# Weight-gradient products moved from the end of a backward pass in among its earlier weight products

## Chip, cores, metric

One core of one Trainium2 chip. The metric is device microseconds (us) of one execution. "Before" is the kernel as found, "after" the changed one. Most executions of one kernel lie within about 1% of each other. Each ratio here compares runs of the same call on the same chip. Where two changed kernels run at different times are set side by side, only their ratios to before are strictly comparable. In "1192 us (1187 to 1196)" the first number is the median and the brackets hold the lowest and highest run.

## The reference, cut to what matters

The program runs two layers of attention and MLP with shared weights, for two rows of activations, forward and backward, and returns the output and nine gradients.

```
# D = 1024, F = 3584, 32 query heads, 4 KV heads of 128, 16384 cached keys, batch 2
x = x + A(layernorm(x))     # attention over a cache, then @ wo
x = x + B(layernorm(x))     # gelu(y @ w1 + b1) @ w2 + b2
x = x + A(layernorm(x))     # same weights again
x = x + B(layernorm(x))
out, vjp = jax.vjp(...)     # gradients of x, k_cache, v_cache, wq, wo, w1, b1, w2, b2
```

A weight gradient is an outer product summed over four rows (two layers, two batch rows). dW2, dW1 and dWo are 23 MB in bf16: little arithmetic, many bytes to store.

## The kernel before

In what follows PE is the matrix engine (TensorE) and PEld its loading of stationary operands, DVE is VectorE, ACT is ScalarE, POOL is GpSimd. PSUM is the memory that TensorE writes to; an "eviction" copies a result from PSUM to the working memory SBUF.

The kernel streams weights and caches (348 MB read, 99 MB written). After 700 us come, in this order:

1. **w1**: for layer 0, w1 is loaded, transposed on TensorE and multiplied by `dh_all` into `dm`;
2. **ln**: two layernorm backwards, with transposes ("turns") of wo rows between their steps, up to `gA_all`;
3. **wo products**: wo times `gA_all`;
4. **loop**: delta of layer 0 and the first pass over kept keys and values, the score loop;
5. **tail**: the rest of the K and V gradients, dWq, and before the change also all of dW2, dW1 and dWo.

In the w1 stage a "push" transposes up to eight blocks into PSUM, copies them to SBUF and multiplies the push of two steps ago:

```
def push(self, wv, j, jj, o0, on):                       # class BwdPipe, cut
    tp = (pt if self.n % 3 else px)([128, 8, 128], BF16, "wtp")
    for o in range(on):
        PE.transpose(tp[:, o, :], wv[:, j, (o0 + o) * 128:(o0 + o + 1) * 128], ident[:])
    wT = ktp.tile([128, 8, 128], BF16, name="wT", tag="kT")
    evac_bf16(wT..., tp..., on * 128)                    # on ScalarE or VectorE
    ...                                                  # then the matmuls of an older wT
```

A gradient "unit" is one product of 4 rows x 128 columns by 4 rows x 512 columns into one PSUM bank, plus one eviction into a 1 MB tile (its "home"), which is stored when full. There are 176 of them: 56 for dW2, 56 for dW1, 64 for dWo.

```
def u(...):                                              # dw_units, cut
    if j == 0 and c0 == 0:
        box["t"] = new_home()
    ps = mx()
    PE.matmul(ps[:], lhsT=xrows[p:p + 4, ...128 columns], rhs=yrows[p:p + 4, ...512 columns],
              start=True, stop=True, tile_position=(p, 0))
    evac_cast(sv_[:, j, c0:c0 + 512], ps[:], 512)
    if j == rb - 1 and c0 + 512 >= ny:
        store(out_of(j0, rb), sv_, box["t"])
```

The stages, cut:

```
_, dmps = w_pass(B_w1, D, F, "dm_ps", gT_bf=dh_all[:, :, lsl(0)])      # w1
wob = Ahead(A_wo, HD, "wob")                                           # loads of wo
dn = ln_bwd(..., lambda: some(rest, 4)); dx = ln_bwd(...)              # ln, with turns between
for j in range(wob.J + 4): ...; wob.products(j - 4, dops, gA_all[...]) # wo products
do_delta(0, pairs(dops, HQ))
by_read = deque(ld.tile(...) for _ in range(NLD - 1))                  # load tiles, NLD = 7
fill = deque(); fill.append(rows_unit(...)); fill.append(... units of dW2, dW1, dWo ...)
for c in range(NCH): ...                                               # score loop
while ...: ...                                                         # tail: takes from fill and late
```

Of the kernel before, what the change touches and what calls it, by code (L numbers as in the profile page):

```python
# [23 lines left out]
def kernel(  # L24
# [50 lines left out]
    NLD = 7  # L75
    WIDE = 32
# [99 lines left out]
    def part_sum(src, n, name):  # L176
        ps = pm_([128, n], F32, name)
        PE.matmul(ps[:], lhsT=onesf[:], rhs=src, start=True, stop=True)
        return ps
# [8 lines left out]
    def col_to_row_f32(colT, J, dram_out, name):  # L188
        row = wrk.tile([2, J * 128], BF16, name=name + "_row", tag="rowout")
        for j0 in range(0, J, 4):  # L190
            ps = pm_([2, 4, 128], F32, name)
            for j in range(4):
                PE.transpose(ps[0:2, j, :], colT[:, j0 + j, :], identf[:])
            V.tensor_copy(out=row[:, j0 * 128:(j0 + 4) * 128], in_=ps[0:2, :, :].rearrange("p a b -> p (a b)"))
        nc.gpsimd.dma_start(dram_out, row[:])
# [57 lines left out]
    class BwdPipe:  # L253


        def __init__(self, out_ps, gT_bf, n_o):
            self.out_ps, self.gT, self.n_o, self.q, self.n = out_ps, gT_bf, n_o, deque(), 0

        def push(self, wv, j, jj, o0, on):
            self.n += 1  # L260
            tp = (pt if self.n % 3 else px)([128, 8, 128], BF16, "wtp")
# [383 lines left out]
    n_all = vec.tile([128, DJ, 4], BF16, name="n_all")  # L645
    o_all = vec.tile([128, HQ, 4], BF16, name="o_all")
    dq_all = vec.tile([128, HQ, 4], BF16, name="dq_all")
    gA_all = vec.tile([128, DJ, 4], BF16, name="gA_all")
    m_all = vec.tile([128, DJ, 4], BF16, name="m_all")
    h_all = vec.tile([128, FJ, 4], BF16, name="h_all")  # L650
    dh_all = vec.tile([128, FJ, 4], BF16, name="dh_all")
    gM_all = vec.tile([128, DJ, 4], BF16, name="gM_all")
# [86 lines left out]
    def attn_out_bwd(l, gT):  # L739
        V.tensor_copy(out=gA_all[:, :, lsl(l)], in_=gT[:])  # L740
        _, dops = w_pass(A_wo, HD, D, "do_ps", gT_bf=gA_all[:, :, lsl(l)])
        return do_delta(l, dops)

    def do_delta(l, dops):
# [5 lines left out]
        doT_bf = vec.tile([128, G, 8], BF16, name=f"doT_bf{l}")  # L750
        V.tensor_copy(out=doT_bf[:], in_=dof[:])
        prod = wrk.tile([128, G, 8], F32, name="dprod")
        V.tensor_tensor(out=prod[:], in0=dof[:], in1=sv["oT"][:], op=ALU.mult)
        dlp = part_sum(prod[:].rearrange("p g r -> p (g r)"), G * 8, "dl_ps")
        rest_ = wrk.tile([128, G * 8], F32, name="dl_rest")
        V.tensor_scalar(out=rest_[:], in0=dlp[:], scalar1=-1.0, scalar2=None, op0=ALU.mult)
# [12 lines left out]
        saved[f"a{l}"]["doT_bf"] = doT_bf  # L769
        return doT_bf  # L770
# [78 lines left out]
    x4 = mlp_out(1, fps[:, 0:DJ * WIDE].rearrange("p (j b) -> p j b", b=WIDE)[:, :, 0:2])  # L849
    col_to_row_f32(x4, DJ, out_0.rearrange("b s d -> (b s) d"), "o0")  # L850
    sv = saved["m0"]
    _, dmps = w_pass(B_w1, D, F, "dm_ps", gT_bf=dh_all[:, :, lsl(0)])
    wob = Ahead(A_wo, HD, "wob")
    for k in range(len(wob.chunks)):
        wob.load(k)
    rest = deque(lambda j=j: wob.row(j) for j in range(wob.J - 4))
    dm = wrk.tile([128, DJ, 2], F32, name="dm_sb")
    V.tensor_copy(out=dm[:], in_=dmps[:])
    dn = ln_bwd(dm[:], sv["y2"][:], sv["rstd2"][:], "dn", lambda: some(rest, 4))
    dx = ln_bwd(dn[:], sv["y1"][:], sv["rstd1"][:], "dx", lambda: some(rest, 4))  # L860
    g1 = vec.tile([128, DJ, 2], F32, name="gM0")
    V.tensor_tensor(out=g1[:], in0=dx[:], in1=g2[:], op=ALU.add)
    V.tensor_copy(out=gA_all[:, :, lsl(0)], in_=g1[:])
    dops = px([128, 512], F32, "wob_b")
    for j in range(wob.J + 4):
        some(rest, 1)
        if j >= wob.J - 4 and j < wob.J:
            wob.row(j)
        if j >= 4:
            wob.products(j - 4, dops, gA_all[:, :, lsl(0)])  # L870
    TP = [pt([128, 8, 128], BF16, "tpm%d" % i) for i in range(2)]
    for t in TP:
        V.memset(t[:].bitcast(F32), 0.0)
    do_delta(0, pairs(dops, HQ))



    rowsA = ld.tile([128, LDW], BF16, name="rowsA", tag="ld")
    rowsB = wrk.tile([128, D], BF16, name="rowsB", tag="rowout")

    def rows_unit(srcs, dst, j0):

        def u():
            tp = mtp()
            n = 0
            for i, (colT, jlo) in srcs.items():
                jn = min(8, colT.shape[1] - jlo)
                n = max(n, jn)
                for j in range(jn):
                    PE.transpose(tp[32 * i:32 * i + 4, j, :], colT[:, jlo + j, :], ident[:], tile_position=(0, 32 * i))  # L890
            lo, hi = 32 * min(srcs), 32 * max(srcs) + 4
            evac_bf16(dst[lo:hi, j0 * 128:(j0 + n) * 128], tp[lo:hi, 0:n, :].rearrange("p a b -> p (a b)"), n * 128)

        return Unit(u)

    X = [px([128, 512], F32, "xm%d" % i) for i in range(4)]
    rot = {"x": 0, "tp": 0}


    by_read = deque(ld.tile([128, LDW], BF16, name="big", tag="ld") for _ in range(NLD - 1))  # L900
    by_store = deque()

    def nxt(what, lst):
        rot[what] += 1
        return lst[(rot[what] - 1) % len(lst)]

    def mx():
        return nxt("x", X)

    def mtp():  # L910
        return nxt("tp", TP)

# [13 lines left out]
    class Unit:  # L926
        def __init__(self, f, home=False):
            self.f, self.home = f, home

        def ready(self):  # L930
            return not self.home or n_free() > 3
# [4 lines left out]
    def dbias(rows, i, n, out_ap, name):  # L936
        p = 32 * i
        row = new_home()
        for c0 in range(0, n, 512):
            ps = mx()  # L940
            PE.matmul(ps[p:p + 1, :], lhsT=ones_bf[p:p + 4, 0:1], rhs=rows[p:p + 4, c0:c0 + 512], start=True, stop=True,
                      tile_position=(p, p))
            evac_cast(row[p:p + 1, c0:c0 + 512], ps[p:p + 1, :], 512)
        store(out_ap.rearrange("(o f) -> o f", o=1), row[p:p + 1, 0:n], row)

    def dw_units(xrows, yrows, i, chunks, y0, ny, out_of):

        p = 32 * i
        box = {}
        units = []  # L950
        for j0, rb in chunks:
            for j in range(rb):
                for c0 in range(0, ny, 512):
                    def u(j0=j0, rb=rb, j=j, c0=c0):
                        if j == 0 and c0 == 0:
                            box["t"] = new_home()
                        sv_ = box["t"][:, 0:rb * ny].rearrange("p (j n) -> p j n", j=rb)
                        ps = mx()
                        PE.matmul(ps[:], lhsT=xrows[p:p + 4, (j0 + j) * 128:(j0 + j + 1) * 128],  # L959
                                  rhs=yrows[p:p + 4, y0 + c0:y0 + c0 + 512], start=True, stop=True, tile_position=(p, 0))  # L960
                        evac_cast(sv_[:, j, c0:c0 + 512], ps[:], 512)
                        if j == rb - 1 and c0 + 512 >= ny:
                            store(out_of(j0, rb), sv_, box["t"])
                    units.append(Unit(u, j == 0 and c0 == 0))
        return units

    def rows_of(out_ap):
        return lambda j0, rb: out_ap[j0 * 128:(j0 + rb) * 128, :].rearrange("(j p) n -> p j n", p=128)

# [18 lines left out]
    def load_next():  # L988
        job = jobs.popleft()
        t = loaded[job] = load_tile()  # L990
# [21 lines left out]

    pump(NLD - 1, 0)

    fill = deque()
    fill.append(rows_unit({0: (gM_all, 0), 1: (m_all, 0), 2: (gA_all, 0), 3: (n_all, 0)}, rowsB, 0))
    for j0 in range(0, HQ, 8):
        srcs = {0: (h_all, j0), 1: (dh_all, j0), 2: (o_all, j0)}
        fill.append(rows_unit({i: v for i, v in srcs.items() if j0 < v[0].shape[1]}, rowsA, j0))
    units = [dw_units(rowsA, rowsB, 0, list(w_chunks(F, D)), 0, D, rows_of(out_8)),  # L1020
            dw_units(rowsB, rowsA, 1, list(w_chunks(D, F)), 0, F, rows_of(out_6))]
    while any(units):
        for u_ in units:
            if u_:
                fill.append(u_.pop(0))
    fill.append(Unit(lambda: dbias(rowsB, 0, D, out_9, "db2"), True))
    fill.append(Unit(lambda: dbias(rowsA, 1, F, out_7, "db1"), True))
    fill.extend(dw_units(rowsA, rowsB, 2, list(w_chunks(HD, D)), 0, D, rows_of(out_5)))
# [5 lines left out]
    for w in "VK":  # L1034
        cols[w] = vec.tile([128, G, 2, 8], BF16, name="cols" + w)
        for k in range(2):
            src = saved["a%d" % k]["qT_bf" if w == "K" else "doT_bf"]
            V.tensor_copy(out=cols[w][:, :, k, :], in_=src[:])
# [82 lines left out]
    def quarter(kv):  # L1121
# [3 lines left out]
        late.append(rows_unit({3: (dq_all, kv * 8)}, rowsA, kv * 8))  # L1125
# [172 lines left out]
```

## Time and profile before

1181.67 us, median of 3 runs (1176.63 to 1184.82), at a mean granted TensorE clock of 0.827 in the profiled run, which took 1184.54 us.

The first view is the page's division of the span into 40 slices of 29.6 us. DMA is the busy share of the DMA engines in tenths, PEclk is the granted TensorE clock in tenths of full speed, GB/s is what the DMA engines moved.

```profile
PEclk9988886597989876989998998987877877786785
DMA  9999999998999989989999939767999999999996
GB/s 370 416 417 417 417 417 395 393 341 365 417 417 413 412 312 416 393 327 414 411 396 383 365 136 398 293 231 296 372 403 420 420 413 418 419 421 418 423 423 267
```

DMA is busy nine tenths or more of almost every slice, and 410 to 423 GB/s recur. The exceptions behind the middle are slices 24, 26, 27 and 28, counted from one (136, 293, 231 and 296 GB/s), that is 680 to 710 us and 740 to 829 us.

The second view gives the busy time of each engine by stretch; I cut the stretches at the stages. The columns are: stretch, its length, then busy us and instruction count of PE, PEld, DVE, ACT and POOL, then clock, DMA share, GB/s. The six rows are w1, ln, a short step from `gA_all` to the first product, wo products, loop, tail.

```profile
core 0: us, PE busy (x) PEld busy (x) DVE busy (x) ACT busy (x) POOL busy (x), PEclk, DMA share, GB/s
711.00:735.40 24.40, 21.93 (x460) 20.45 (x461) 10.81 (x20) 9.17 (x16) 0.71 (x1) 0.89 1.03 400
735.40:743.00 7.60, 6.37 (x92) 5.51 (x90) 5.51 (x24) 3.52 (x6) 0.00 (x0) 1.00 0.94 344
743.00:744.10 1.10, 1.02 (x16) 0.90 (x16) 0.64 (x2) 0.44 (x1) 0.00 (x0) 1.00 0.24 82
744.10:760.20 16.10, 16.06 (x412) 15.67 (x409) 7.27 (x11) 6.01 (x11) 0.00 (x0) 1.00 0.81 290
760.20:779.70 19.50, 13.32 (x246) 7.92 (x247) 10.55 (x33) 6.60 (x15) 0.58 (x1) 0.77 0.48 196
779.70:1182.80 403.10, 350.77 (x4505) 210.22 (x4503) 295.85 (x505) 276.01 (x527) 57.28 (x97) 0.75 0.96 389
```

In w1 the DMA is full (share 1.03, where 1 or a little over is full; 400 GB/s), though PE is also 90% busy. The wo products run at 290 GB/s and the loop at 196. The tail is bound by bytes: 403 us at 389 GB/s and a DMA share of 0.96, though the clock is only 0.75. Its loads wait for stores to give tiles back, as the largest row of the DMA queue's own waits in the tail shows (total us, times, longest):

```profile
SPq L997 <- DMA out_dram<-big: 103.1, 16, 17.5
```

### The profile page before, as it was taken

The page shows a single profiled execution, that of the slowest core. Times are in us where ns is not written, and L with a number is a line of the kernel's source. Part 1 is how long each engine was busy: PE and PEld are TensorE (multiplying, and loading weights), DVE is VectorE, ACT ScalarE, POOL GpSimd, SP SyncE. Part 2 cuts the span into 40 slices and gives each one's busy share as a digit, 9 for nine tenths or more (in the row PEclk, how much of TensorE's full clock was granted, in tenths as well). Part 3 has the DMA queues.
Part 4 walks back from the last instruction along what each step waited for, and adds up shares of the span by engine and source line. Part 5 has one row for each costly group of instructions (what it writes and reads, how often), then busy time and mean ns, then how long its engine had stood idle before and what let it go on. Part 6 is the DMA issues. An engine that isn't in the chain of part 4 may idle for free. (4 is left out here: it accounts for less than half of the span.)

```text
span 1182.8 us, 40678 instructions
## 1 busy us (share of the span) xinstructions
PE 981.7 (83%) x17981; PEld 754.3 (64%) x17981; DVE 606.4 (51%) x1264; ACT 538.2 (46%) x1366; POOL 63.9 (5%) x113
## 2 busy tenths in 40 slices
PE   4989795488879876899798988888988889999885
PEld 3867673488767756887676788755555554555552
DVE  1544351233535423444243334567877877786774
ACT  0544341022535421334233323366766867685773
POOL 0000000000000000000000000001111111111111
PEclk9988886597989876989998998987877877786785
DMA  9999999998999989989999939767999999999996
GB/s 370 416 417 417 417 417 395 393 341 365 417 417 413 412 312 416 393 327 414 411 396 383 365 136 398 293 231 296 372 403 420 420 413 418 419 421 418 423 423 267
DMA packets 89133, 449.35 MB, mean 380 GB/s; under 512 B 7026, under 2 KB 7026, under 8 KB 49788
## 3 DMA queue, kind: packets, MB, share of 16 engines
q1 hardware_dynamic: 72204, 348.17, 73.9%
q0 software_dynamic: 16752, 98.59, 20.3%
q8 instruction: 140, 2.29, 0.8%
q14 instruction: 37, 0.30, 0.1%
HBM read 348.14 MB, written 98.58 MB: 378 GB/s over the span
## 5 line engine op out<-in xcount | busy, mean ns | idle before, releaser
L148 ACT COPY kT<-tp 128x512 int32<-128x512 int32 x181 | 106.3, 587 | 266.0 <-PE tp L379 258.2
L151 DVE COPY kT<-tp 128x1024 bf16<-128x1024 bf16 x187 | 128.1, 691 | 152.7 <-PE tp L379 143.1
L379 PE MATMUL tp<-ident,kv_K 128*128 128x128 bf16 x1728 | 144.7, 233 | 4.6 <-DMA kv_K<-in_A_k_cache_dram 4.0
L379 PEld LDWEIGHTS <-kv_K 128*128 128x128 bf16 x1728 | 109.9, 104 | 5.2 <-DMA kv_K<-in_A_k_cache_dram 5.1
L159 DVE CAST big<-xm 128x512 bf16<-128x512 f32 (+1 forms) x140 | 91.0, 685 | 30.3 <-PE xm L1100 15.9
L156 ACT CAST big<-xm 128x512 bf16<-128x512 f32 (+1 forms) x157 | 85.7, 593 | 25.1 <-PE xm L959 15.1
L521 PEld LDWEIGHTS <-kT 128*128 128x128 bf16 x2048 | 76.7, 98 | 28.7 <-issue 22.9
L521 PE MATMUL sc<-qT_bf,kT 128*128 128x8 bf16 x2048 | 92.2, 171 | 0.7 <-issue 0.7
L263 PE MATMUL wtp<-ident,wt 128*128 128x128 bf16 x928 | 77.0, 231 | 3.6 <-issue 2.3
L297 PEld LDWEIGHTS <-wt 128*128 128x128 bf16 x1696 | 49.1, 103 | 46.4 <-issue 15.3
L485 ACT ACTIVATE e_all<-sc,negm 128x64 bf16<-128x64 f32 x256 | 77.1, 343 | 1.3 <-DVE negm L480 1.1
L379 PE MATMUL tp<-ident,kv_V 128*128 128x128 bf16 x864 | 69.9, 227 | 7.7 <-DMA kv_V<-in_A_v_cache_dram 6.3
L159 DVE CAST keepK<-xm 128x512 bf16<-128x512 f32 x95 | 61.7, 684 | 18.8 <-PE xm L1100 13.6
L405 PE MATMUL acc_all<-kv_V,e_all 128*16 128x256 bf16 x864 | 46.5, 295 | 29.2 <-DMA kv_V<-in_A_v_cache_dram 16.2
L148 ACT COPY wT<-wtp 128x512 int32<-128x512 int32 (+1 forms) x60 | 34.5, 576 | 78.2 <-PE wtp L263 63.4
L151 DVE COPY wT<-wtp 128x1024 bf16<-128x1024 bf16 (+1 forms) x64 | 40.5, 636 | 52.0 <-PE wtp L263 48.7
L156 ACT CAST keepK<-xm 128x512 bf16<-128x512 f32 x102 | 54.8, 592 | 19.7 <-PE xm L1100 18.9
L263 PEld LDWEIGHTS <-wt 128*128 128x128 bf16 x928 | 58.9, 103 | 4.4 <-issue 2.9
L379 PEld LDWEIGHTS <-kv_V 128*128 128x128 bf16 x864 | 54.6, 102 | 9.8 <-DMA kv_V<-in_A_v_cache_dram 7.3
L159 DVE CAST keepV<-xm 128x512 bf16<-128x512 f32 (+1 forms) x78 | 50.8, 685 | 18.8 <-PE xm L1100 14.8
L156 ACT CAST keepV<-xm 128x512 bf16<-128x512 f32 (+1 forms) x94 | 51.0, 594 | 19.8 <-PE xm L1100 16.8
L485 ACT ACTIVATION_READ_ACCUMULATOR e_all<-sc,negm 128x1 f32 x256 | 59.8, 234 | 0.0
(325 smaller groups left out, 1762.7 us busy)
## 6 DMA issues: line engine op xcount, KB each, us to landing
kv_K<-in_A_k_cache_dram SPq DMA_DIRECT2D x81, 1024.0 KB, 12.9
kv_V<-in_A_v_cache_dram SPq DMA_DIRECT2D x81, 1024.0 KB, 11.9
out_dram<-big POOLq DMA_DIRECT2D x36, 1024.0 KB, 17.0
wt<-in_A_wo_dram SPq DMA_DIRECT2D x32, 1024.0 KB, 11.1
wt<-in_B_w_dram SPq DMA_DIRECT2D x32, 896.0 KB, 14.4
out_dram<-keepK POOLq DMA_DIRECT2D x22, 1024.0 KB, 17.3
out_dram<-keepV POOLq DMA_DIRECT2D x18, 1024.0 KB, 17.2
wt<-in_A_wq_dram SPq DMA_DIRECT2D x16, 1024.0 KB, 9.1
```

Source lines behind the costliest of these rows:

```text
L148: S.copy(out=dst.bitcast(I32), in_=src.bitcast(I32))
L151: V.tensor_copy(out=dst, in_=src)
L156: S.copy(out=dst, in_=src)
L159: V.tensor_copy(out=dst, in_=src)
L263: PE.transpose(tp[:, o, :], wv[:, j, (o0 + o) * 128:(o0 + o + 1) * 128], ident[:])
L297: PE.matmul(fps[:, jo, :].rearrange("p (a b) -> p a b", b=2), lhsT=wv[:, j, jo * 128:(jo + 1) * 128], rhs=xT_bf[:, j0 + j, :].unsqueeze(1) ...
L379: PE.transpose(tp[:, j, :], cv[:, b * 8 + j, :], ident[:])
L405: PE.matmul(self.acc[cg:cg + 16, :], lhsT=coef(u), rhs=self.cv[:, t:t + 2, :].rearrange("p t d -> p (t d)"), start=False, stop=True, tile_ ...
L485: S.activation(out=e_all[:, g, f * half:(f + 1) * half, l, h, :], in_=sc[g][f][:, h, :].rearrange("p (a b) -> p a b", b=2), func=ACT.Exp, ...
L521: PE.matmul(sc[g][f][:, :, t % TH], lhsT=kT[:, j, :], rhs=q_bf[:, g, :], start=True, stop=True)
```

## The change

The intent: the tail is full of bytes and the stages before it have some room, so the gradient products and their stores go there. Three load tiles become homes early. Two units are "fed" after each w1 push and each wo turn, one after each wo product, three per step of the score loop. So that neighbouring units use different parts of the TensorE array, each operand's rows are spread over four strips of partitions (0, 32, 64, 96). The row transposes of out_0 go from ahead of w1 to ahead of the wo products. Delta of layer 0 is divided: the scaled gradient comes before the loop, the sum inside its first step. The transposes of w1 also lose the third PSUM bank that they took in turn before. No byte is added or removed. The diff, cut to its core:

```diff
+    by_read, by_store = deque(), deque(ld.tile([128, LDW], BF16, name="home", tag="ld") for _ in range(NHOME))
 ...
+                    if split == "x":
+                        p, xo, yo = 32 * (jj % 4), jj // 4 * 128, c * 512
+                    else:
+                        p, xo, yo = 32 * (c % 4), jj * 128, c // 4 * 512
+                    PE.matmul(ps[:], lhsT=x[p:p + 4, xo:xo + 128], rhs=y[p:p + 4, yo:yo + 512], start=True, stop=True,
+                              tile_position=(p, 0))
 ...
+    fill.extend(dw_units(hr, gMr, list(w_chunks(F, D)), D, rows_of(out_8), "x"))
+    feed(4)
     x4 = mlp_out(1, ...)
-    col_to_row_f32(x4, DJ, out_0.rearrange("b s d -> (b s) d"), "o0")
+    feed(4)
 ...
-    _, dmps = w_pass(B_w1, D, F, "dm_ps", gT_bf=dh_all[:, :, lsl(0)])
+            for o0 in range(0, FJ, 8):
+                pipe.push(wv, j, j0 + j, o0, min(8, FJ - o0))
+                feed(2)
 ...
+    LEAD = 4 * (NLD - NHOME)
+    def turned(j):
+        wob.row(j)
+        feed(2)
 ...
+    for j in range(wob.J):
+        if j >= LEAD // 2 and j + LEAD // 2 < wob.J:
+            wob.row(j + LEAD // 2)
+        wob.products(j, dops, gA_all[:, :, lsl(0)])
+        feed(1)
 ...
-    do_delta(0, pairs(dops, HQ))
+    prod = do_scaled(0, pairs(dops, HQ), cols["V"][:, :, 0, :])
 ...
     for c in range(NCH):                                   # score loop
+        if c == 0:
+            qv()
+            delta(0, prod, mx())
 ...
+        feed(3)
```

## The prediction

> **What bounds the kernel now.** The slices of the page show DMA at 0.9 or more of its time almost everywhere, at about 418 GB/s: the kernel is bound by moved bytes (449 MB). Summing the windows view, about 180 MB move after 700 us; at 418 GB/s that is 431 us, but it takes 482 us, so some 50 us of DMA time is idle there. It lies at 700-706 us (5), 740-750 (149 GB/s: 6), 765-790 (14), 800-825 (9, clock 0.67) and the drain after 1150 (10). The w1 products run from 713.7 to 735.5 us, wo turns and products to 760, delta to 764 (timeline). dW2, dW1 and dWo (23 MB, 55 us of DMA) all come after 811 us, where DMA is already full: loads wait for stores to free tiles (the DMA queue's waits: over 300 us on stores).
>
> **What changes.** No bytes are added or removed. 176 dW units (one 4x128x512 product, one eviction: 0.59 us on ACT or 0.69 on DVE, 372 ns on PE, partly overlapped) and their stores move forward. Counting the feeds: 8 units before w1, 64 among its 32 pushes, 32 among the first 16 wo turns, about 32 in the wo products, 12 in the score loop; some 30 stay in the tail. About 148 units, 18.5 MB, leave the tail: 44 us at 418 GB/s.
>
> **What it costs.**
> - w1: 22 us becomes 33-37: 64 evictions (41 us) plus the wT ones (18) over two engines is 30 us, at 80-90% filling. The Trainium skill (TensorEngine Tiling (Array Packing), PSUM Bottleneck) says that tiling speeds TensorE, not eviction; I expect that here: four strips help PE little, the evictions set the pace.
> - rows transposes and eight units before w1: about 3 us.
> - the 16 turns with both layernorm backwards: 18 us; out_0's transposes (3.5 us) now stand before the wo products.
> - wo products: 28-30 us, since only four tiles hold weights and the last four chunks are loaded only as products free them.
> So wo products end near 798-805 us instead of 760: 38-45 us later. DMA is near full in w1, but idles some 15-20 us in the layernorm chain and the wo products (8 there before).
>
> **What it gains back.** The tail loses 44 us. The gap at 765-780 mostly closes: delta waits inside the first score step, V gradients and dWo stores flow at once, and no clearing or rows units stand in the way (10-15 us of idle gone). One more tile is free for loads. Four instead of six loads are prefetched (-5 us). The drain is unchanged.
>
> **Sum.** 1182 + 42 - 44 - 12 (gap and rows) = about **1168 us**, range **1150 to 1187**. Faster by over 2%: 0.30; within 2%: 0.64; slower by over 2%: 0.06. So most of the 44 us is paid back by slower w1 and wo stages.
>
> **What would show it.** DMA rate in the w1 stage stays above 380 GB/s though it lasts 12 us or more longer; ACT and DVE busy there go from about 45% to 80% or more; wo products end near 800 us; a DMA trough (below 300 GB/s) in the layernorm chain and the start of the wo products, with PE waiting for the fifth wo chunk; no trough below 100 GB/s in the score loop; tail still at 415-420 GB/s, ending about 10-15 us earlier.
>
> **What would make it wrong.** Faster: evictions and PE overlap better, so w1 ends at 30 us and products by 790 (then 1150). Slower: a unit's eviction waits for its home's store (three homes, 17 us to landing in the tail) and blocks the in-order engines and so the products; or the tail turns out bound by PE (88-92% busy there at a clock near 0.75) rather than by bytes, so that taking stores out gives little.

## The result, and the profile after

After ran in 1219.27 us (1216.36 to 1225.12, 4 runs) against 1179.15 us (1176.32 to 1184.82, 4 runs) for before. Ratios here are the mean time of one kernel's fast runs over that of the other's from the same rounds, so not quite the ratio of those medians: 1.034, 95% interval 1.028 to 1.040. The change made the kernel slower; the prediction was wrong.

The 40 slices of after (30.4 us each):

```profile
PEclk9988795678898857999889965565977997796795
DMA  9999999989999989999999388457999999999965
GB/s 372 418 420 419 419 418 396 390 312 420 419 418 419 390 356 400 354 405 413 396 392 373 128 311 299 186 200 281 374 407 416 424 424 420 424 423 421 417 277 208
```

The same six stages of after:

```profile
702.30:761.20 58.90, 56.22 (x637) 37.58 (x626) 32.43 (x53) 33.22 (x60) 6.60 (x9) 0.54 0.82 303
761.20:781.50 20.30, 20.30 (x136) 12.07 (x134) 8.85 (x30) 15.15 (x29) 2.13 (x4) 0.50 0.58 234
781.50:788.50 7.00, 6.09 (x38) 3.27 (x36) 3.97 (x6) 3.37 (x6) 0.53 (x1) 0.50 0.32 131
788.50:834.90 46.40, 39.67 (x486) 24.86 (x483) 17.93 (x26) 15.94 (x28) 3.71 (x6) 0.57 0.62 216
834.90:857.40 22.50, 19.27 (x267) 8.99 (x268) 12.74 (x35) 11.07 (x23) 1.86 (x3) 0.50 0.75 278
857.40:1217.90 360.50, 281.69 (x4328) 180.88 (x4328) 248.15 (x434) 230.04 (x442) 43.69 (x76) 0.79 0.94 387
```

Differences of the two profiles, stage by stage in us:

| | start of w1 | w1 | ln | step | wo products | loop | tail | end |
|---|---|---|---|---|---|---|---|---|
| before | 711.0 | 24.4 | 7.6 | 1.1 | 16.1 | 19.5 | 403.1 | 1182.8 |
| after | 702.3 | 58.9 | 20.3 | 7.0 | 46.4 | 22.5 | 360.5 | 1217.9 |
| difference | -8.7 | +34.5 | +12.7 | +5.9 | +30.3 | +3.0 | -42.6 | +35.1 |

The tail gave back what was expected. The four stages ahead of the loop took 83.4 us more. (The start of w1 is not the change's doing for certain: over my twelve runs, whose code up to there is nearly that of after, it lay anywhere between 704 and 709 us. And each stage is read from one execution: the profiled one of before, at 1184.54 us, was 5 us above before's median.)

What stands out is the clock. In w1 PE is busy 56.2 of 58.9 us, at 0.54 of full speed; before it was 0.89. In stretches of 5 us it reads as follows. First after: in w1, in ln, two in the wo products, and at the start of the tail:

```profile
715.00:720.00 5.00, 5.00 (x52) 3.58 (x51) 2.63 (x5) 2.78 (x6) 0.77 (x1) 0.50 0.92 366
775.00:780.00 5.00, 5.00 (x35) 3.10 (x34) 3.12 (x5) 3.27 (x7) 0.53 (x1) 0.50 0.52 210
795.00:800.00 5.00, 0.51 (x1) 0.00 (x1) 0.38 (x1) 0.59 (x1) 0.00 (x0) 0.50 1.01 356
810.00:815.00 5.00, 4.92 (x102) 3.64 (x100) 2.57 (x4) 2.77 (x5) 0.00 (x0) 1.00 0.60 213
860.00:865.00 5.00, 4.43 (x77) 3.07 (x78) 4.22 (x8) 3.61 (x8) 0.00 (x0) 1.00 0.99 391
```

Then before, in w1 and at the wo products:

```profile
720.00:725.00 5.00, 5.00 (x123) 4.89 (x119) 2.23 (x4) 2.81 (x5) 0.00 (x0) 1.00 1.01 394
745.00:750.00 5.00, 5.00 (x121) 4.92 (x118) 2.21 (x5) 2.32 (x4) 0.00 (x0) 1.00 0.46 107
```

In after, PE shows no idle time in these stretches of w1 and ln, and yet keeps half its clock. Apart from 7 us it is back at 1.00 only from about 858 us on, when the tail begins (whose mean is 0.79). (By stage it is 0.50 to 0.57 from w1 to the loop.) In those 7 us the trace shows what was different: from 806.7 to 811.4 us PE ran transposes and wo products alone, no gradient product, and at 810 us the clock went to 1.00; then a gradient product came every 1.1 us or so, PE idled for 0.6 us, and at 817 us the clock was at 0.50 again. In before the clock is 1.00 in both. The page's groups, restricted to w1, show the cost for single operations (busy us, mean ns). First after (lines between left out), then before:

```profile
L265 PE MATMUL wtp<-ident,wt 128*128 128x128 bf16 x224 | 29.7, 310 | 0.0
...
L955 PE MATMUL xe<-gMr,hr 4*128 4x512 bf16 x56 | 16.4, 569 | 1.7 <-ACT home L157 0.9 <-ACT hr L149 0.7
```

```profile
L263 PE MATMUL wtp<-ident,wt 128*128 128x128 bf16 x224 | 18.1, 227 | 0.0
```

The same 224 transposes have a mean of 310 ns instead of 227, and a gradient product lasts 569.

### The profile page after: what moved, and what is told of

It reads as the page before. It is cut to its first block, busy times and chain, and to the rows that moved or that the text cites. A ratio compares the mean times of both kernels' runs of the same rounds, so it can differ in the third digit from the quotient of the medians.

```text
span 1217.9 us, 41059 instructions
## 1 busy us (share of the span) xinstructions
PE 995.2 (82%) x18149; PEld 761.5 (63%) x18149; DVE 600.4 (49%) x1261; ACT 545.2 (45%) x1377; POOL 63.8 (5%) x113
## 3 DMA queue, kind: packets, MB, share of 16 engines
q0 software_dynamic: 16752, 98.59, 19.8%
## 5 line engine op out<-in xcount | busy, mean ns | idle before, releaser
L265 PE MATMUL wtp<-ident,wt 128*128 128x128 bf16 x928 | 91.2, 256 | 3.3 <-issue 2.0
L265 PEld LDWEIGHTS <-wt 128*128 128x128 bf16 x928 | 68.4, 115 | 18.2 <-issue 16.8
L299 PEld LDWEIGHTS <-wt 128*128 128x128 bf16 x1696 | 49.0, 103 | 45.0 <-issue 14.7
L381 PE MATMUL tp<-ident,kv_V 128*128 128x128 bf16 x864 | 67.4, 222 | 7.4 <-DMA kv_V<-in_A_v_cache_dram 6.4
L407 PE MATMUL acc_all<-kv_V,e_all 128*16 128x256 bf16 x864 | 46.4, 294 | 29.1 <-DMA kv_V<-in_A_v_cache_dram 17.7
L157 ACT CAST home<-xe 128x512 bf16<-128x512 f32 (+1 forms) x84 | 47.7, 586 | 46.6 <-PE xe L955 40.0
L149 ACT COPY wT<-wtp 128x512 int32<-128x512 int32 (+1 forms) x58 | 32.9, 568 | 61.4 <-PE wtp L265 51.7
L160 DVE CAST keepK<-xm 128x512 bf16<-128x512 f32 x80 | 51.5, 684 | 16.7 <-PE xm L1155 11.5
L149 ACT COPY kT<-tpm 128x512 int32<-128x512 int32 x65 | 38.7, 595 | 45.2 <-PE tpm L1305 45.0
L160 DVE CAST home<-xe 128x512 bf16<-128x512 f32 (+1 forms) x57 | 39.2, 690 | 37.1 <-PE xe L955 35.0
L157 ACT CAST keepK<-xm 128x512 bf16<-128x512 f32 x88 | 47.3, 592 | 14.7 <-PE xm L1155 10.7
L160 DVE CAST big<-xm 128x512 bf16<-128x512 f32 x64 | 41.5, 684 | 23.0 <-PE xm L1155 21.0
## 6 DMA issues: line engine op xcount, KB each, us to landing
kv_V<-in_A_v_cache_dram SPq DMA_DIRECT2D x81, 1024.0 KB, 12.7
```

The source lines that it names most:

```text
L149: S.copy(out=dst.bitcast(I32), in_=src.bitcast(I32))
L157: S.copy(out=dst, in_=src)
L160: V.tensor_copy(out=dst, in_=src)
L299: PE.matmul(fps[:, jo, :].rearrange("p (a b) -> p a b", b=2), lhsT=wv[:, j, jo * 128:(jo + 1) * 128], rhs=xT_bf[:, j0 + j, :].unsqueeze(1) ...
L381: PE.transpose(tp[:, j, :], cv[:, b * 8 + j, :], ident[:])
L407: PE.matmul(self.acc[cg:cg + 16, :], lhsT=coef(u), rhs=self.cv[:, t:t + 2, :].rearrange("p t d -> p (t d)"), start=False, stop=True, tile_ ...
```

## Experiments

Theory A: the thin products (4 of 128 rows) keep TensorE's granted clock at one half although it is busy, and PE so becomes the pace of w1, ln and wo. The Trainium skill ("TensorE: Matmul & The Clock Gate", Part 1, What's actually happening) says that the clock is throttled by default and released by activity, with half and full as the two states, and that a sustained busy window of about 3.4 us is enough to release it. That an instruction which is busy all the time might not count fully is not in that section; that is what had to be tested.

Rival B: it is the switching between the strips and the whole array. The skill ("TensorEngine Tiling (Array Packing)", Key Properties) says that a change of tiling mode drains TensorE; on such a story the clock is a symptom.

Rival C: evictions and homes are the pace, as the prediction held, and the low clock is only what an engine gets that waits.

Theory D, besides, which the expectations name from run 8 on: feeding early is a loss in itself, because w1's DMA was already full.

### 1. Products over all 128 rows (results of dW wrong, on purpose)

```diff
-PE.matmul(ps[:], lhsT=x[p:p + 4, xo:xo + 128], rhs=y[p:p + 4, yo:yo + 512], start=True, stop=True,
-          tile_position=(p, 0))
+PE.matmul(ps[:], lhsT=x[:, xo:xo + 128], rhs=y[:, yo:yo + 512], start=True, stop=True)
```

The number of products, evictions, homes and bytes is unchanged. (One small memset of rows that nothing else writes is added; runs 5, 6 and 7 have it too.)

> Changed kernel, but every dW product multiplies all 128 rows of its operand tiles instead of 4 (dW2, dW1, dWo, dWq come out wrong on purpose; same count of products, columns, evictions, bytes). Theory A (the clock): products that use 4 of 128 rows leave the array looking idle, so TensorE is granted half its clock (0.55 in w1, 0.50 to 0.57 to the end of the wo products) and paces these stages. Then here: granted clock above 0.9 in the w1 stage, w1 stage 34 to 40 us instead of 59, wo products 30 to 36 instead of 47, total 1170 to 1190 us. Rival B (switching between 32-row strips and the whole array costs time by itself): faster too, since nothing switches any more, so this run alone does not part A from B. Rival C (evictions and waits for home tiles set the pace): no change, 1219 us, w1 59 us.

Measured: 1191.94 us (1186.55 to 1196.29) beside 1179.93 (1177.25 to 1183.22) for before, ratio 1.009 (1.006 to 1.013). Stages w1 and wo products, then the two groups of w1 again:

```profile
708.60:757.80 49.20, 40.99 (x646) 28.75 (x635) 32.21 (x55) 32.22 (x60) 6.65 (x10) 0.93 0.97 360
776.60:812.20 35.60, 27.74 (x486) 21.00 (x484) 17.75 (x26) 15.64 (x28) 3.10 (x6) 0.81 0.68 229
```

```profile
L265 PE MATMUL wtp<-ident,wt 128*128 128x128 bf16 x224 | 19.1, 229 | 0.0
L955 PE MATMUL xe<-gMr,hr 128*128 128x512 bf16 x56 | 17.8, 389 | 4.4 <-DVE home L160 3.0 <-ACT hr L149 0.7 <-ACT home L157 0.5
```

The clock is 0.93 in w1 and the products, though 32 times as many rows, last 389 ns instead of 569. Some 27 of the 40 us are gone. But w1 still takes 49 us where theory A had forecast 34 to 40, the total misses its range by 2 us, and now the DMA is full in w1 (0.97), at 360 GB/s.

### 2. Products over 32 rows (wrong, on purpose)

```diff
-lhsT=x[p:p + 4, ...], rhs=y[p:p + 4, ...]
+lhsT=x[p:p + 32, ...], rhs=y[p:p + 32, ...]        # same tile_position=(p, 0)
```

> Changed kernel with every dW product on all 32 rows of its strip instead of 4 (dW wrong on purpose); the strips and the switching stay. A, if what counts is how many rows work: between the changed kernel and the full-row run, clock in w1 0.6 to 0.9, total 1185 to 1212 us. B: no change, 1219 us, clock in w1 0.55, since the switching is the same. C: no change.

Measured: 1214.01 us (1205.63 to 1216.42), ratio 1.027 (1.023 to 1.031). w1:

```profile
704.30:764.20 59.90, 56.81 (x641) 37.99 (x627) 32.42 (x53) 33.12 (x60) 6.58 (x9) 0.53 0.80 296
```

Nearly as after: filling one strip helps neither the clock nor w1. This is what B and C had forecast; theory A, in the form that more rows give more clock step by step, missed both its clock and its total.

### 3. No products until the wo products have ended (wrong, on purpose)

```diff
+if late_stage:
     PE.matmul(ps[:], lhsT=x[p:p + 4, ...], rhs=y[p:p + 4, ...], start=True, stop=True, tile_position=(p, 0))
-evac_cast(sv_[:, j, c * 512:(c + 1) * 512], ps[:], 512)
+evac_cast(sv_[:, j, c * 512:(c + 1) * 512], ps[:] if late_stage else ACCT[:], 512)
```

Evictions and stores stay where after has them; they read an idle PSUM bank.

> Changed kernel without the dW products up to the end of the wo products: their evictions, stores and waits for home tiles stay, but read the idle accumulator bank (those dW wrong on purpose). A and B: clock 0.9 to 1.0, w1 stage 32 to 38 us (evictions then set the pace: about 30 us of busy time on each of two engines), wo products 28 to 34, total 1165 to 1185 us. C: w1 stays near 59 us and the total near 1219 us.

Measured: 1196.42 us (1191.73 to 1200.89), ratio 1.013 (1.010 to 1.017). w1:

```profile
704.40:754.90 50.50, 32.14 (x579) 29.40 (x568) 30.48 (x54) 30.92 (x61) 6.95 (x10) 0.71 0.97 364
```

With the products gone and all evictions left, w1 falls from 59 to 50 us, as with full rows. So rival C can claim at most 50 us of w1, not the 59. The forecast of A and B (32 to 38 us in w1, total 1165 to 1185) was missed too; only the wo products, at 30.6 us, lie in it. PE is now idle 18 us of w1, so its clock of 0.71 says little; the DMA share is 0.97.

### 4. Delta in one part again (correct)

```diff
-    prod = do_scaled(0, pairs(dops, HQ), cols["V"][:, :, 0, :])
+    delta(0, do_scaled(0, pairs(dops, HQ), cols["V"][:, :, 0, :]))
 ...
-            delta(0, prod, mx())
```

> Changed kernel with the layer-0 delta computed in one part before the score loop, as the kernel before has it (results right). The score loop then waits for the chain of some 11 small VectorE steps (about 2.5 us). All theories: 1219 to 1223 us; the two-part delta is worth 1 to 3 us and is not the cause of the loss.

Measured: 1221.93 us (1220.26 to 1224.87), ratio 1.034 (1.032 to 1.037). After had 1219.27 with the same ratio of 1.034. This part of the change is worth 3 us at most and cannot be told from nothing.

### 5. Half the array: 64 rows (wrong, on purpose)

```diff
+h = 64 * (p // 64)
+PE.matmul(ps[:], lhsT=x[h:h + 64, xo:xo + 128], rhs=y[h:h + 64, yo:yo + 512], start=True, stop=True,
+          tile_position=(h, 0))
```

> Changed kernel with every dW product on 64 rows (a half of the array as its tile; dW wrong on purpose). Parts A from B together with the 68-row run, which has nearly as many rows but takes the whole array as its tile. A (what counts is how many rows work): 64 and 68 rows give the same clock in w1 within 0.1 and totals within 8 us of each other. B (what counts is the change of tile size between these products and the transposes around them): 64 rows stay at a clock near 0.54 in w1 and at 1210 to 1220 us.

Measured: 1207.38 us over four runs that fall in two pairs: 1196.40 and 1200.06, and 1214.70 and 1219.42, the latter at a mean clock of 0.827 and 0.821 instead of 0.847 and 0.848 and counted as slow. Ratio of the fast pair 1.014 (1.008 to 1.019). w1 of the profiled, fast run:

```profile
705.20:757.20 52.00, 47.74 (x642) 28.79 (x631) 32.43 (x55) 32.95 (x60) 6.58 (x9) 0.86 0.92 343
```

In this run the products still change the tiling between whole array and half array again and again, and the clock is 0.86 all the same. Rival B, as the cause of the low clock, does not survive that. The total alone would not decide it: the two slow runs lie where B had forecast, they left no profile, and what slowed them is not known. In the fast run's own trace the clock fell after PE had idled from 743.6 to 746.5 us and came back only at 760, with PE busy throughout; other falls in runs 1, 5, 6 and 7 ended after 3 to 6 us. So 64 rows may stand near a limit; one such fall does not prove it.

### 6. 68 rows, whole array (wrong, on purpose)

```diff
+PE.matmul(ps[:], lhsT=x[0:68, xo:xo + 128], rhs=y[0:68, yo:yo + 512], start=True, stop=True)
```

> Changed kernel with every dW product on 68 rows, from row 0, so that the whole array is its tile (dW wrong on purpose). A: same as 64 rows. B: as the full-row run: clock about 0.9 in w1, total 1188 to 1196 us.

Measured: 1193.21 us (1189.84 to 1197.02) beside 1181.38 (1177.58 to 1185.58), ratio 1.010 (1.006 to 1.014). All six stages, since this is after with its clock mended:

```profile
704.20:753.00 48.80, 42.21 (x642) 29.84 (x630) 31.98 (x53) 32.41 (x60) 6.59 (x10) 0.90 0.97 363
753.00:768.00 15.00, 13.96 (x148) 9.55 (x145) 8.90 (x30) 14.74 (x30) 2.11 (x4) 1.00 0.79 303
768.00:772.10 4.10, 2.52 (x24) 1.43 (x22) 3.59 (x7) 2.29 (x5) 0.53 (x1) 1.00 0.66 269
772.10:805.90 33.80, 26.77 (x486) 20.20 (x483) 17.73 (x26) 15.65 (x28) 3.10 (x6) 0.85 0.72 245
805.90:826.90 21.00, 17.12 (x267) 9.08 (x267) 12.73 (x36) 11.80 (x24) 2.29 (x4) 0.76 0.89 319
826.90:1188.10 361.20, 283.19 (x4328) 181.42 (x4327) 247.60 (x434) 230.04 (x441) 43.73 (x77) 0.83 0.94 390
```

The clock is not quite full even here (0.90 in w1, 0.85 in the wo products). In runs 1, 5, 6 and 7 it fell to 0.50 too, most often after PE had stood idle for 2 us or more, but it came back; in after and run 2 it stayed at 0.50 to the end of w1. The effect goes with the rows that an instruction occupies:

| rows of a product | 4 (after) | 32 | 64 | 68 | 128 |
|---|---|---|---|---|---|
| clock in w1 | 0.54 | 0.53 | 0.86 | 0.90 | 0.93 |
| w1, us | 58.9 | 59.9 | 52.0 | 48.8 | 49.2 |
| whole kernel, us | 1219.3 | 1214.0 | 1196 to 1200, or 1215 to 1219 | 1193.2 | 1191.9 |

The size of the tile goes the same way (4 and 32 rows are addressed as a tile of 32 rows, 64 as one of 64, 68 and 128 as the whole array). A product of 4 rows on the whole array, which would part rows from tile size, was not run.

### 7. 68 rows of zeros (wrong, on purpose)

Rows, or what is really multiplied? The last run of the study gave run 6 a stationary operand of zeros:

```diff
+zero_x = const.tile([128, 128], BF16, name="zero_x"); V.memset(zero_x[:], 0.0)
-PE.matmul(ps[:], lhsT=x[0:68, xo:xo + 128], rhs=y[0:68, yo:yo + 512], start=True, stop=True)
+PE.matmul(ps[:], lhsT=zero_x[0:68, :], rhs=y[0:68, yo:yo + 512], start=True, stop=True)
```

> As the run with 68 rows (wrong results, on purpose), but the stationary operand of every dW product is a tile of zeros, so the matmuls have the same shape, rows and timing and multiply by nothing. If the granted clock follows the rows that an instruction occupies, w1 again takes 48 to 50 us at a clock of 0.88 to 0.95 and the kernel 1188 to 1198 us. If the clock follows what is really multiplied (values, not rows), w1 takes 56 to 60 us at a clock of 0.5 to 0.6 and the kernel 1210 to 1220 us.

Measured: 1194.51 us (1187.68 to 1199.24) beside 1179.67 (1175.56 to 1186.49), ratio 1.012 (1.005 to 1.018). w1, and a stretch of 5 us in it, which compares with those of after:

```profile
707.40:760.10 52.70, 44.86 (x642) 31.49 (x631) 32.24 (x54) 32.59 (x60) 6.59 (x10) 0.84 0.90 337
720.00:725.00 5.00, 5.00 (x82) 3.72 (x79) 4.37 (x8) 4.33 (x8) 0.76 (x1) 1.00 0.78 281
```

The total lies in the range for rows; w1 (52.7 us at 0.84) missed both ranges. Its clock stands much nearer to that of rows. It was at 0.50 three times, each time after PE had idled for 1.8 to 2.7 us (713 to 719, 737 to 743, 754 to 757 us), and came back each time, which in w1 of after it never did. Multiplying by zeros is enough to bring the clock back; whether zeros delay the return, one profile does not show. So operands padded with zeros to more rows, which would be correct, should keep the clock as well; that padded version was not built.

### 8. Nothing fed before the wo products have ended, seven tiles for wo (correct)

This tests theory D. The four-strip layout, two-part delta and new loop of the change stay; the feeding, and with it the transposes that make the rows, moves back into loop and tail (four units per loop step instead of three, one in the first).

```diff
-                feed(2)                    # after each w1 push
 ...
-        feed(2)                            # after each wo turn
 ...
-        feed(1)                            # after each wo product
 ...
-        feed(3)
+        feed(1 if c == 0 else 4)           # score loop
```

In this run the three home tiles also stay with the weights until the wo products have ended, so that 28 wo rows are turned ahead instead of 16. (To make room in SBUF, a few scratch tiles share their places and one kind has two buffers instead of three; all late kernels, runs 8 to 10, have this.)

> Changed kernel with nothing fed before the wo products have ended: the w1 and wo stages have seven weight tiles and no dW product, as before; the four-strip rows, the two-part delta and the reordered score loop with 12 dW2 products in it stay, the other dW products follow in the tail. Results right. My account (clock, a full DMA in w1 and the three home tiles are the whole loss): clock 0.9 to 1.0 and 24 us in w1, wo products 16 to 18 us, total 1172 to 1179 us, at or a little under the kernel before. Rival (the new score loop, the rows or the delta cost time too): above 1185 us.

Measured: 1184.27 us (1178.66 to 1186.65) beside 1181.38, ratio 1.001 (0.996 to 1.006): between my range and the rival's, so neither is borne out. The step from `gA_all` to the first product:

```profile
740.20:750.70 10.50, 8.47 (x120) 7.08 (x118) 4.13 (x6) 5.42 (x10) 0.00 (x0) 1.00 0.04 13
```

w1 is back at 22.4 us, at 404 GB/s. But in this arrangement 28 of the 32 turns stand ahead of the first product and hold all seven tiles: the step takes 10.5 us, with 13 GB/s moved. That was a fault of my edit and spoils the comparison with the next run.

### 9. The same, four tiles for wo and three homes as in after (correct)

```diff
-    LEAD = 4 * NLD
+    LEAD = 4 * (NLD - NHOME)
-    by_read, by_store = deque(), deque()
+    by_read, by_store = deque(), deque(ld.tile(... name="home" ...) for _ in range(NHOME))
```

The order of turns and products goes back to that of after as well.

> The run with late dW products, but three of the seven weight tiles kept away from w1 and wo as in the changed kernel. My account: w1 24 to 28 us, wo products 26 to 32 us because the last four wo chunks load only as products free tiles, total 10 to 16 us above the seven-tile run. Rival (only the clock costs, tiles are free): within 3 us of the seven-tile run.

Measured: 1169.52 us (1168.36 to 1172.06), ratio 0.990 (0.986 to 0.993). I had expected 10 to 16 us more than run 8, and the rival the same within 3; it is 15 us less. Four tiles do not starve the wo products (14.3 us). All six stages:

```profile
708.10:730.50 22.40, 21.70 (x447) 20.61 (x446) 8.32 (x16) 10.11 (x18) 0.00 (x0) 0.93 1.03 404
730.50:739.50 9.00, 8.01 (x121) 7.24 (x119) 3.01 (x19) 7.26 (x14) 0.00 (x0) 1.00 1.01 371
739.50:742.10 2.60, 1.83 (x26) 1.39 (x24) 0.68 (x1) 1.33 (x3) 0.00 (x0) 1.00 0.16 59
742.10:756.40 14.30, 14.30 (x390) 14.07 (x391) 5.80 (x12) 5.26 (x9) 0.71 (x1) 1.00 0.86 318
756.40:776.20 19.80, 16.57 (x328) 9.82 (x328) 12.69 (x33) 11.47 (x23) 1.90 (x3) 0.83 0.60 226
776.20:1170.30 394.10, 331.25 (x4593) 199.26 (x4591) 292.18 (x501) 272.36 (x520) 55.82 (x95) 0.77 0.97 397
```

Against run 6, on the same chip and with a good though not equal clock in both, w1 through wo products are 53.4 us shorter (22.4 + 9.0 + 2.6 + 14.3 for 48.8 + 15.0 + 4.1 + 33.8), and loop and tail 31.7 us longer (19.8 + 394.1 for 21.0 + 361.2). That is theory D with its numbers: feeding early costs more than it returns, even with the clock mostly mended. By the medians run 9 is 24 us faster than run 6. What is left of the low clock in run 6's wo products, and the scratch tiles, are in this difference and were not separated.

### 10. The late kernel with more in its loop (correct)

The loop still shows 226 GB/s. Two variants and a repeat of run 9.

```diff
         feed(1 if c == 0 else 4)
+        if c > 0:
+            pump(NLD + 3, 2)               # ask for loads of the tail inside the loop
```

> This is the late kernel (nothing of dW1, dW2 or dWo before the wo products have ended) in which two already loaded turns may be asked for per key group in the score loop, so that the 10 us of the loop in which the late kernel's DMA moved only about 140 GB/s are filled by loads of the tail. If the loop's hole is worth what it looks like (226 GB/s over 19.8 us against some 400, so about 3.4 MB, or 8 us at the tail's 395 GB/s), the time is 1160 to 1166 us. Rival: the loads come earlier but the turns' own TensorE work and tiles hold the loop up, and the time stays at 1168 to 1173 us.

```diff
-        feed(1 if c == 0 else 4)
+        feed(1 if c == 0 else 8)
```

> The late kernel with eight instead of four units of dW products per key group in the score loop. If TensorE at full clock has room in the loop, twelve more home tiles leave the tail early and the time is 1164 to 1169 us; the rival, that the loop is then held up by evictions and stores and only shifts the work, gives 1168 to 1174 us. In both cases it stays below the kernel before, because w1 and the wo products are untouched.

> The late kernel once more, unchanged, on this chip, so that the two variants can be compared with it within one call: 0.986 to 0.994 of the kernel before, that is 1167 to 1174 us.

Measured beside 1179.26 us (1177.93 to 1182.96) for before: the repeat 1172.51 (1170.35 to 1173.36), ratio 0.994 (0.991 to 0.996), as expected; with early loads 1169.34 (1168.23 to 1171.79), ratio 0.992 (0.989 to 0.994); with eight units 1177.57 (1174.52 to 1178.61), ratio 0.998 (0.995 to 1.000). The loop of the early-loads kernel, then that of the eight-units kernel:

```profile
754.70:774.80 20.10, 16.48 (x326) 9.58 (x319) 12.76 (x32) 11.46 (x23) 1.90 (x3) 0.83 0.63 240
```

```profile
753.50:780.10 26.60, 21.52 (x338) 10.49 (x339) 16.82 (x38) 14.73 (x30) 2.68 (x4) 0.66 0.73 263
```

The early loads did not fill the loop (240 GB/s), and the gain of 8 us that I had expected is not there; the two late kernels cannot be told apart. Eight units per step lengthen the loop to 26.6 us, drop the clock to 0.66 and cost 5 us against the repeat, more than I had allowed the rival. Both kernels with four units beat before, by under 1%, and after.

## Why the prediction was wrong

**What held.** The bound of the tail: 18.5 MB should leave it for 44 us; it lost 42.6 us (32 units stayed there, as counted), and it ended as full of bytes as it had been (387 GB/s over all, 416 to 424 in its middle slices). The prediction had feared that PE sets the tail's pace; run 1 speaks against that: its tail has a clock of 0.85 instead of 0.79 and takes 362.1 us instead of 360.5. A DMA trough and a wait of PE for the fifth wo chunk were announced for the wo products, and are there: in after, PE does 0.5 us of work between 795 and 800 us, and this row of its waits in the wo products names a load of wo. But the reason given for 28 to 30 us, that four tiles starve these products, fails: with four tiles and nothing fed (run 9) they take 14.3 us. The row:

```profile
PE turn L315 <- DMA wt<-in_A_wo_dram: 5.8, 2, 5.2
```

**The step that failed first: "four strips help PE little, the evictions set the pace", with 33 to 37 us for w1.** The Trainium skill ("TensorEngine Tiling (Array Packing)", PSUM Bottleneck) says that tiling speeds TensorE but not PSUM evacuation, and I made that the pace. The evictions kept their length in after's w1 (587 ns on ACT, 691 on DVE), as that section lets one expect, but they were not the pace: ACT and DVE are busy 33.2 and 32.4 of 58.9 us in w1, 56% and 55% and not the 80% I had announced, and PE 95%. Their evictions mostly wait for PE. My costing took its PE durations from the trace of before, 372 ns for a unit's product; in after's w1 it took 569. The thin products keep the clock from coming back, from about 708 to 858 us but for 7 us at 810; runs 1, 2, 5, 6 and 7 tie this to the rows they occupy or to the size of their tile. Mending it takes 1219 to 1192 or 1193 us: about 26 us of the 51 between prediction and result. Even then w1 takes 49 us, with ACT and DVE 65% busy and the DMA full, so evictions do not set the pace there either. "DMA rate in the w1 stage stays above 380 GB/s" was false by the same step: 303. And the wo products, announced to end near 800 us, ended at 834.9.

**The second: the price of feeding early, full clock or not.** With the clock mended (run 6), w1, ln, step and wo products take 101.7 us; before they took 49.2. That is 52.5 us more, where I had allowed 38 to 45. (Counted from the start of the kernel, run 6's wo products end at 805.9 us, 1 us after the announced range; but its w1 started 7 us earlier than before's.) w1 had no room: its DMA share was 1.03 before. Run 6 moves 363 GB/s x 48.8 us = 17.7 MB there against 9.0 MB in run 9 (404 x 22.4): 8.7 MB for 26.4 us, at 328 GB/s. Over the stages from w1 to the loop, the same sums give 16.8 MB more for 54.6 us, or 308 GB/s. In the tail they save 32.9 us, for 15.6 MB by the same sums (397 x 394.1 less 390 x 361.2). So a megabyte costs 3.2 us where it went and frees 2.1 us where it came from. Why the rate among the products stays at 360 rather than 400 and more, with home stores and weight loads in one stretch, I did not isolate. The profile's queue table narrows it: for the share of DMA time that they took in w1, the stores of run 6 moved at 400 GB/s (8.16 MB in 41.8% of 48.8 us), its loads at 358 (9.44 MB in 54.0%), and those of run 9 at 395 (9.00 MB in 101.7% of 22.4 us). It is the loads that got slower. The skill ("Trainium Kernel Development and Optimization", Key Constraints) says that DMAs of all issuing queues run on the same 16 engines and interleave; the full share agrees with that, but it does not explain the lower rate. In run 1 two rows of the waits in w1 say that evictions wait for home stores:

```profile
ACT home L157 <- DMA out_dram<-home: 8.4, 4, 3.4
...
DVE home L160 <- DMA out_dram<-home: 3.8, 2, 3.6
```

These 12 us of engine waits are there at a clock of 0.93; the prediction named the homes as a risk and did not cost it.

**The third: I counted the same gain twice.** "The gap at 765-780 mostly closes ... 10-15 us of idle gone" was subtracted beside the 44 us. Idle DMA time that fills with bytes is a gain only where these bytes leave another stage, and for the gradients that is already the 44 us. Run 6 shows it: its loop moves 319 instead of 196 GB/s, so the gap does largely fill, and yet the stage is 21.0 us long instead of 19.5. Of the 2.9 MB more that move there, 1.4 MB are stores. The other 1.5 MB are loads, and the tail's own loads did not become fewer for it (59.8 MB for 58.7). That term was -12 and came out at +1.5. (Nor did "no trough below 100 GB/s in the score loop" hold: from 844 to 848 us after moved 4 GB/s.)

The account of the 51 us: by medians about 26 us are the clock (after less run 6), and 25 remain between run 6 and the prediction. By the profiles of before and run 6 these are some 10 for the stages (52.5 for 42), 13 for the gap (+1.5 for -12) and 2 for the tail (-41.9 for -44), while w1 started 7 us earlier in run 6's profile. One kernel's runs spread over 7 to 9 us and each stage is read from one profile (before's is 5 us above its median, run 6's 3 us below), so only the first of these terms is far outside the noise.

**What the rest of the change is worth.** Run 9 is the change without early feeding, and is 7 to 12 us below before (ratio 0.990, and 0.994 in the repeat). By the first profile 9 of them are in the tail (394.1 for 403.1). 12 units (1.5 MB, 4 us at 397 GB/s) moved into the loop; the rest is spread over the new rows, loop order and tile use, which I did not separate. By the 2% by which the prediction counted, before and run 9 are the same.

**Open.** Whether it is the rows or the tile size that counts; where the limit between 32 and 64 rows lies and whether 64 is just at it; what the two slow runs of run 5 were; whether zero-padded, correct products behave like run 7; and why loads in w1 slow down beside the stores.

## What to carry to other kernels

Before moving work into an earlier stage, look at what that stage is full of: w1 was full of DMA, and moving stores there from another full stage cost more than it gained. When you mix products that use few rows (here 4 or 32) into a stage, cost every TensorE instruction of the stage at half clock as well, and read the clock in short stretches of the trace: busy all the time at half speed looks like a full engine. And when a plan fills idle time with moved work, count the gain once, either as idle that disappears or as work that leaves.

## What the Trainium skill lacked or had wrong

- "TensorE: Matmul & The Clock Gate", Part 1: it ties full clock to busy time alone (about 3.4 us of it). Here PE was recorded busy 5.00 of 5 us, stretch after stretch in w1 and ln, at a clock of 0.50, with products of 4 or 32 rows among whole-array ones; 64, 68 and 128 rows gave 0.86, 0.90 and 0.93 in the same stage, and 68 rows with a zero operand 0.84. What counts as activity is missing.
- The same page, Part 4 (PE-mode transpose): it says that transposes do not count as busy in the same way. In w1 of before, half of the matmuls are transposes (224 of 448 on weights) and the clock is 1.00 from 717 us on; in after's wo products it came back at 810 us after 3.3 us in which transposes took some four fifths of PE's time. A mixture with whole-array products was enough. No run here had transposes alone.
- The same page's advice to avoid idle gaps of about 3 us ("Why this matters for your kernels") was not enough: after had fewer gaps than before in w1 (95% busy for 90%) and the lower clock. With 128 and 68 rows most falls did follow gaps, of 2.2 to 3.2 us (run 1 at 736 and 750, run 6 at 732 and 745 us).
- "TensorEngine Tiling (Array Packing)": nothing on the clock. It presents row strips as a way to use the array better; strips used one at a time, 4 or 32 rows each, went with neighbouring 128x128 transposes 309 to 310 ns long instead of 227.
- "DMA: Bandwidth & Descriptors", Specifications: the table's limit of about 358 GB/s from HBM for a core is no limit for this one core, whose slices show 410 to 423 GB/s over long stretches; its later section on bandwidth, which has single-core figures of that size, agrees.
